# One exponential in forty by a polynomial on VectorE and GpSimd, in a four-layer attention kernel

## The chip, the cores and the metric

The kernel runs on one core of a Trainium2 chip. A core has a matrix engine (PE, TensorE), a vector engine (DVE, VectorE), an activation engine (ACT, ScalarE), a general engine (POOL, GpSimd) and a queue that issues transfers (SP). Each works through its own list of instructions in order and waits for the others by semaphores. The metric is device time in microseconds (us), the median of several runs.

## What is computed

The input `x` is 2048 tokens by 1024 features in bf16. Four layers follow one another, each with a layer norm and a residual add: A, B, A, B, with the same weights for both A and for both B.

```
x = x + A(layernorm(x));  x = x + B(layernorm(x));  x = x + A(layernorm(x));  x = x + B(layernorm(x))

A: q, k, v = split(x @ wqkv)                       # 32 heads of 32
   phi(t) = [softmax(t @ w_phi), softmax(-(t @ w_phi))]
   o = phi(q) (phi(k)^T v) / (phi(q) sum(phi(k)) + 1e-6);   return o @ wo
B: scores = q k^T / sqrt(32)                       # 32 heads, 2048 x 2048 each
   p = softmax(scores);   return (p v) @ wo
```

Layer B is full attention: per layer 32 x 2048 x 2048 exponentials. The kernel does not subtract a row's maximum; it sums `exp(scores)` by a product with ones, in the same matmuls that sum `exp(scores) v`, and divides at the end.

## The kernel before

All order is written by a planner in the program itself. Every instruction, or small group of them, is an `op` with an engine, an assumed duration, dependencies, buffers and a priority (a number; a smaller one goes first). `Sched.run` (line 143) plays these out: whenever an engine is free, it takes the ready op of smallest priority whose buffers can be had. The order that results is then emitted, and on the chip each engine follows it whatever the true durations are. Buffers come from one arena in SBUF, with a limit on how many of each class may live (`QUOTA`, line 245), and from the eight banks of PSUM.

**The two A layers** are done per chunk of 512 tokens: keys and their state (`a_keys`, line 569), then queries (`a_queries`, 708), the output product with the residual add (`a_out`, 783; the add is line 792) and the layer norm for B (`layernorm`, 441). The layer norm squares the chunk on ScalarE (line 454), lets PE average `x` and its squares by a product with a matrix of 1/1024 (line 397), and normalizes on VectorE (lines 487 and 491). For three chunks of the second A layer this is done beside the first attention, with squares on VectorE (`alone`).

**Attention** (`attention`, line 908) is a run of 2048 units for each B layer. A unit is one matmul of scores (line 937): 128 keys by 512 queries of one head, over 32 rows of PE, one bank of PSUM. Units go in 32 turns (`turns`, line 1029): turn = a chunk of 512 queries `qc` and a group of four heads `g`; in it `pp` (2), `d` (8 blocks of keys) and `j` (4) give 64 units. Three units at a time fill half of the six score banks; one ScalarE instruction takes the exponential of all three (line 943) into a buffer of class `E`, of which five may live. PE then multiplies each by `v` and by ones (line 972) and accumulates over the 16 blocks of keys in bank 6. Bank 6 is single: when a `pp` is done, VectorE copies it out (line 986) before the next may begin. At the end of a turn two transfers swap halves, and VectorE takes reciprocals (line 1016) and multiplies (line 1020).

Bank 7 (`FIL`) is the eighth bank. Through it go, beside attention, the projections that later turns need (keys, queries, values: `b_k`, `b_q`, `q_away`, `b_v`; VectorE empties the bank, lines 816, 824, 840), the output products (`b_o`, `b_last`) and, in the first attention, three chunks of the next A layer's keys. Where PE has been busy less than 75% of the last 3.4 us of the plan, the planner puts in a padding matmul to bank 7 (line 1177), if bank 7 is free and no projection uses it.

GpSimd makes two memsets (line 662) and 64 small casts (line 607), none of them in the second attention.

The factor 1/sqrt(32) is applied where VectorE copies `q` out of PSUM (lines 824 and 840).

Of the kernel before, what the change touches and what calls it, by code (L numbers as in the profile page):

```python
# [12 lines left out]
BF16 = mybir.dt.bfloat16  # L13
F32 = mybir.dt.float32

EPS_LN = 1e-5
# [16 lines left out]
class Op:  # L33
    __slots__ = ("eng", "dur", "lat", "fn", "bufs", "prio", "mode", "ndep", "out", "t", "start", "seq")

    def __init__(self, eng, dur, lat, fn, bufs, prio, mode, seq):
        self.eng, self.dur, self.lat, self.fn, self.bufs = eng, dur, lat, fn, bufs
        self.prio, self.mode, self.seq = prio, mode, seq
        self.ndep, self.out, self.t, self.start = 0, [], 0.0, None

# [5 lines left out]
class Sched:  # L46
    def __init__(self, sbuf_bytes, quota):
        self.ops = []
        self.quota = quota
        self.live = {}  # L50
        self.free = [(0, sbuf_bytes)]
        self.bank_used = [False] * 8
        self.peak = 0
        self.total = sbuf_bytes
        self.queue = {}
        self.idle = None

# [85 lines left out]
    def run(self):  # L143
# [17 lines left out]
        front = 0  # L161
        recent = []
        started = {}
        for o in self.ops:
# [3 lines left out]
        while left:  # L168
            moved = False
            for e in engines:  # L170
                if busy[e] > t + 1e-9 or not ready[e]:
                    continue
                skipped = []
                pick = None
                while ready[e] and len(skipped) < 60:
                    item = heapq.heappop(ready[e])
                    if item[0] <= todo[front] + WINDOW and self._alloc(item[2].bufs):
                        pick = item[2]
                        break
                    skipped.append(item)  # L180
                for s in skipped:
                    heapq.heappush(ready[e], s)
                if pick is None and e == "PE" and self.idle is not None and self.live.get("S", 0):

                    recent = [r for r in recent if r[1] > t - SPELL]
                    worked = sum(r[1] - max(r[0], t - SPELL) for r in recent)
                    if worked < KEEP * SPELL and not self.live.get("fil", 0) and not self.bank_used[7]:
                        pick = Op("PE", MM, LAT["PE"], self.idle, (Buf("ps", 0, "idle", [(7,)]),), 0.0, "c", 0)
                        pick.bufs[0].left = 1
                        self.queue["idle"] = [list(pick.bufs), 0]  # L190
                        assert self._alloc(pick.bufs)
                        left += 1
                if pick is None:
                    continue
                if e == "PE":
                    recent.append((t, t + pick.dur))
                d = pick.dur
                if pick.mode is not None:
                    if mode[e] is not None and mode[e] != pick.mode:
                        d += SWITCH  # L200
                    mode[e] = pick.mode
                pick.start = t
                if pick.fn is not self.idle:
                    started[pick.prio] = started.get(pick.prio, 0) + 1
                while front < len(todo) - 1 and started.get(todo[front], 0):
                    started[todo[front]] -= 1
                    front += 1
                busy[e] = t + d
                order.append(pick)
                left -= 1  # L210
                moved = True
                n += 1
                heapq.heappush(events, (t + d, n, pick, True))
                n += 1
                heapq.heappush(events, (t + d + pick.lat, n, pick, False))
            if moved:
                continue
            if not events:
                stuck = [(o.prio, o.eng, [(b.cls, b.at) for b in o.bufs]) for e in engines for _, _, o in ready[e]][:8]
                raise AssertionError(f"nothing can start at {t:.1f}: {left} left, {stuck}, live {self.live}")  # L220
            t = events[0][0]
            while events and events[0][0] <= t + 1e-9:
                _, _, o, own = heapq.heappop(events)
                if not own:
                    for b in o.bufs:
                        b.left -= 1
                        if b.left == 0:
                            self._release(b)
                for x in o.out:

                    if own != (x.eng == o.eng and x.eng not in ("SP", "AQ")):
                        continue
                    x.ndep -= 1
                    if x.ndep == 0:
                        heapq.heappush(ready[x.eng], (x.prio, x.seq, x))
# [11 lines left out]
         "lnt": 6, "lnw": 2, "lnw1": 1, "eq": 8, "ns": 4, "cw": 6, "hl": 6, "oc": 2, "slab": 7, "slabk": 3, "fin": 4,  # L247
         "rs": 8, "pkf": 1, "part": 8, "w2r": 1}
SPELL = 3.4
KEEP = 0.75  # L250


# [4 lines left out]
def dve_us(n):  # L257
    return n / 960 + 0.15
# [6 lines left out]
def kernel(  # L265
# [18 lines left out]
    assert D == 1024 and S % C512 == 0  # L284
    inv_sqrt_dh = float(DH**-0.5)

# [15 lines left out]
    onesD = const.tile([P, P], BF16, tag="onesD")  # L302
    ones_bf = const.tile([P, DH], BF16, tag="ones")
    J_bf = const.tile([P, P], BF16, tag="J")
    ident = const.tile([P, P], BF16, tag="ident")
# [8 lines left out]
    nc.vector.memset(onesD[:], 1.0 / D)  # L314
    nc.vector.memset(ones_bf[:], 1.0)
    nc.vector.memset(J_bf[:], 0.0)
    nc.vector.memset(eps[:], EPS_LN)
# [122 lines left out]

    def layernorm(c, prio, banks, alone=False):

# [5 lines left out]
        parts = [deps_x(c)[2 * i:2 * i + 2] for i in range(4)]  # L448
        for h in range(2 if alone else 4):
            hs = slice(4 * h, 4 * h + 4)  # L450
            if not alone:
                hs = slice(2 * h, 2 * h + 2)
                halves.append(op(
                    "ACT", act_us(1024), lambda hs=hs: nc.scalar.activation(  # L454
                        out=xv()[:, hs, :], in_=xT[:, hs, csl(c)], func=ACT.Square),
                    parts[h], [xb], prio))
            else:
# [6 lines left out]
        if not alone:  # L464
            mb.with_ = (qb,)
        m = mmgroup(mb, mv, lambda po: onesD[:], lambda po: xT[:, po, csl(c)], (), parts, [], prio)
        q = mmgroup(qb, qv, lambda po: onesD[:], lambda po: xv()[:, po, :], [m],
                    [halves[0], None, halves[1], None] if alone else halves, [xb], prio + 0.01)
        if alone:
# [348 lines left out]
    def b_q(g, c, prio, w, banks):  # L818
# [5 lines left out]
        cp = op("DVE", dve_us(512), lambda: nc.vector.tensor_scalar(  # L824
            out=q_v()[:, 0, :], in0=pv(), scalar1=inv_sqrt_dh, scalar2=None, op0=ALU.mult), [m], [pb, q_b], prio)
        return q_b, q_v, q_swap(q_b, q_v, cp, prio)
# [6 lines left out]
    def q_away(g, c, prio, w, banks):  # L833
# [6 lines left out]
        cp = op("DVE", dve_us(512), lambda: nc.vector.tensor_scalar(  # L840
            out=a_v(), in0=pv(), scalar1=inv_sqrt_dh, scalar2=None, op0=ALU.mult), [m], [pb, a_b], prio)
        return dma(prio, lambda: nc.sync.dma_start(out=qd_v[:, c - 2, g, :], in_=a_v()), [cp], [a_b], kb=128)
# [64 lines left out]

    def attention(base, kT, vT, q_of, gate):

# [4 lines left out]
        ]  # L914
        first = {}
        ex_of, e_of = {}, {}
        n = 0
        i = 0
        while i < len(units):
# [14 lines left out]
            def sfn(grp=grp, s_v=s_v):  # L934
# [8 lines left out]
            ex = op("ACT", act_us(w * C512), lambda s_v=s_v, e_v=e_v, w=w: nc.scalar.activation(  # L943
                out=e_v()[:, 0:w * C512], in_=s_v(), func=ACT.Exp), [so], [s_b, e_b], prio - 3)
            for x, u in enumerate(grp):
# [5 lines left out]
        if True:  # L951
            for qc, g in turns:
                T = []
                end = (qc, g) == turns[-1]
                for pp in range(2):
                    a_b, a_v = ps("acc", [(6,)])
                    last = None
                    for d in range(8):
                        prio = base + 10 * pos[(qc, g)] + 5 * pp + 0.5 * d
                        for u in range(2):  # L960
# [18 lines left out]
                            if e_of[us[1]][0] is not ebs[0]:  # L979
                                ebs.append(e_of[us[1]][0])  # L980
                            last = op("PE", 0.225, fn, flat([last, ex_of[us[0]], ex_of[us[1]], v_done[kc % 4]]),
                                      [a_b, v_b, *ebs], prio - 1, mode="c")
                    if end and pp:
                        break
# [67 lines left out]
    for layer in range(2):  # L1052
# [13 lines left out]
        for c in chunks:  # L1066
            xnA[c] = layernorm(c, base + 10 * c - 9 if base + c else -16.0, ANY)
            a_keys(c, base + 10 * c, wk_s, wv_s, kv, ANY)
# [47 lines left out]
        for g in range(G):  # L1116
            pr = at + 10 * pos[(0, g)]
            w = slab("w2", pr - 11, B_w[:, :, g * P:(g + 1) * P], P) if g else wq0
            for qc in range(NC):
# [3 lines left out]
                else:  # L1123
                    away = q_away(g, qc, pr + 2 + 6 * (qc - 2), w, FIL)
                    q_of[(qc, g)] = q_back(g, qc, at + 10 * pos[(qc, g)] - 12, away)
        oTs, last_s = attention(at, kT, vT, q_of, gate)
        if last:
# [50 lines left out]
    sch.idle = idle  # L1178

    for o in sch.run():  # L1180
        o.fn()
# [30 lines left out]
```

## Time and profile before

| | us |
|---|---|
| median of 3 runs | 2554.63 |
| lowest and highest | 2552.54, 2556.16 |
| the profiled execution | 2554.77 |
| its span, first to last instruction | 2553.0 |

| stretch of the span | what | PE busy | DVE busy | ACT busy | POOL busy |
|---|---|---|---|---|---|
| 0 to 400 | first A layer | 361 | 291 | 189 | 13 |
| 400 to 1363 | first attention | 881 | 408 | 945 | 10 |
| 1363 to 1618 | rest of the second A layer | 240 | 171 | 130 | 3 |
| 1618 to 2542 | second attention | 843 | 269 | 915 | 0 |
| 2542 to 2553 | last output rows | 4 | 6 | 1 | 0 |

The mean granted clock of TensorE is 0.985 of full speed. Times are microseconds from the first instruction, and busy time is the time in which at least one instruction of that engine ran. PE's ends are modelled and padding matmuls count as busy, so its share says little; ScalarE's and VectorE's can be read as they stand. In a line of a group the columns are: line, engine, operation, output and inputs, shapes, count, then busy time and mean duration in ns, then the idle time just before these instructions and what ended it. In a timeline the columns are start, duration, engine, line, operation.

### The profile page before, as it was taken

The numbers are of one execution on the slowest core, as the hardware profiler recorded it, in microseconds if no ns is written. First come the engines' busy times: TensorE is split into PE (matmuls) and PEld (weight loads), VectorE is DVE, ScalarE is ACT, GpSimd is POOL, SyncE is SP. The second block draws the span as 40 slices with busy tenths as digits, with TensorE's granted clock in tenths as the row PEclk, the third lists the DMA queues.
The fourth block names the chain that finished last, engine by engine and source line by source line (L and its number), as shares of the span: only waits on it lengthen the run. The fifth ranks groups of instructions, "written<-read, shape, count | busy, mean of one in ns | idle before, by whom it ended". The sixth has DMA issues, their size and how long they took to land.

```text
span 2553.0 us, 60236 instructions
## 1 busy us (share of the span) xinstructions
PE 2329.9 (91%) x26714; PEld 882.9 (35%) x26780; DVE 1144.7 (45%) x1632; ACT 2181.1 (85%) x1945; POOL 25.8 (1%) x72
## 2 busy tenths in 40 slices
PE   6899999999898998899898999999998898889888
PEld 3443443333322333333333344333332233333333
DVE  5997653333322245655646766333333222212124
ACT  5325647999999999999996555799999999999998
POOL 0000000000000000000000000000000000000000
PEclk9999999999998999999999999999999899999999
DMA  9020011111121222222323001111121011001000
GB/s 215 1 75 1 5 38 46 35 35 44 40 64 38 53 53 70 75 64 69 117 71 102 1 5 38 36 45 35 37 67 30 20 33 43 20 18 33 18 20 26
DMA packets 185270, 117.21 MB, mean 46 GB/s; under 512 B 103345, under 2 KB 175025, under 8 KB 184241
## 3 DMA queue, kind: packets, MB, share of 16 engines
q1 hardware_dynamic: 183952, 111.26, 16.3%
q8 instruction: 209, 3.42, 0.6%
q10 hardware_dynamic: 1056, 2.10, 0.2%
q14 instruction: 53, 0.43, 0.1%
HBM read 62.46 MB, written 15.73 MB: 31 GB/s over the span
## 4 chain that ended last, share of the span: by engine, by line
ACT 53%; PE 26%; issue 11%; DVE 8%; SPq 1%; DMA 1%; ACTq 0%; DVEq 0%; another core or an unknown queue 0%
ACT arena L943 51%; PE psum L397 13%; PE psum L401 4%; PE psum L972 3%; PE psum L937 3%; DVE arena L593 2%; DVE arena L602 1%; PE psum L757 1%; DVE arena L491 1%; DVE arena L487 1%; ACT arena L589 1%; SPq L432 1%; DVE arena L596 1%; DVE arena L639 0%; PE psum L702 0%
## 5 line engine op out<-in xcount | busy, mean ns | idle before, releaser
L943 ACT ACTIVATE arena<-psum 128x1536 bf16<-128x1536 f32 (+1 forms) x1366 | 1844.4, 1560 | 29.1 <-PE psum L937 23.6
L972 PE MATMUL psum<-arena 128*32 128x512 bf16 x4096 | 712.7, 390 | 13.5 <-ACT arena L943 11.6
L972 PE MATMUL psum<-arena,ones_bf 128*32 128x512 bf16 x4096 | 714.1, 391 | 0.0
L937 PE MATMUL psum<-arena 32*128 32x512 bf16 x4096 | 537.8, 387 | 135.5 <-ACT arena L943 127.3
L401 PE MATMUL psum<-arena 128*32 128x512 bf16 x8256 | 582.5, 382 | 13.8 <-DVE arena L840 2.1
L397 PE MATMUL psum<-arena 128*128 128x512 bf16 x1973 | 468.6, 382 | 26.5 <-DVE arena L491 5.5
L937 PEld LDWEIGHTS <-arena 32*128 32x128 bf16 x4096 | 181.7, 91 | 643.8 <-issue 632.1
L401 PEld LDWEIGHTS <-arena 128*32 128x32 bf16 x8256 | 213.0, 96 | 222.1 <-issue 74.2
L397 PEld LDWEIGHTS <-arena 128*128 128x128 bf16 x2032 | 193.2, 98 | 268.5 <-issue 50.2
L986 DVE COPY arena<-psum 128x512 f32<-128x512 f32 x126 | 86.9, 690 | 431.3 <-PE psum L972 428.0
L972 PEld LDWEIGHTS <-arena 128*32 128x32 bf16 x4096 | 167.7, 94 | 283.0 <-issue 259.3
L1016 DVE RECIPROCAL arena<-arena 128x128 f32<-128x128 f32 x248 | 212.8, 913 | 85.7 <-DMA arena<-arena 82.8
L816 DVE CAST arena<-psum 128x512 bf16<-128x512 f32 x112 | 77.4, 691 | 283.5 <-PE psum L401 280.3
L972 PEld LDWEIGHTS <-ones_bf 128*32 128x32 bf16 x4096 | 162.1, 94 | 70.1 <-issue 58.7
L401 PE MATMUL psum<-xT,onesD 128*32 128x512 bf16 x2172 | 179.7, 382 | 0.6 <-DVE xT L876 0.3
L589 ACT ACTIVATE arena<-psum 128x512 bf16<-128x512 f32 x80 | 42.6, 603 | 110.7 <-PE psum L397 58.8
L454 ACT ACTIVATE arena<-xT 128x1024 bf16<-128x1024 bf16 x52 | 54.6, 1060 | 73.2 <-DVE xT L792 59.2
L719 ACT ACTIVATE arena<-psum 128x512 bf16<-128x512 f32 x128 | 69.8, 598 | 38.2 <-PE psum L397 32.2
L602 DVE TENSOR_TENSOR arena<-psum,arena 128x1024 bf16<-128x1024 f32 x64 | 78.3, 1224 | 43.6 <-PE psum L401 39.4
L1020 DVE TENSOR_TENSOR arena<-arena 64x512 bf16<-64x512 f32 x124 | 85.0, 686 | 10.1 <-PE psum L972 5.7
L487 DVE TENSOR_TENSOR arena<-xT,arena 128x1024 f32<-128x1024 bf16 x64 | 77.7, 1218 | 22.7 <-ACT arena L476 22.4
L593 DVE TENSOR_REDUCE arena<-arena 128x32 f32<-128x1024 bf16 x64 | 77.6, 1213 | 19.1 <-ACT arena L589 15.0
(89 smaller groups left out, 1051.8 us busy)
## 6 DMA issues: line engine op xcount, KB each, us to landing
arena<-arena SPq DMA_DIRECT2D x124, 128.0 KB, 2.3
arena<-in_A_wqkv_dram SPq DMA_DIRECT2D x10, 1024.0 KB, 5.7
arena<-in_B_wqkv_dram SPq DMA_DIRECT2D x32, 256.0 KB, 3.3
arena<-arena SPq DMA_DIRECT2D x256, 32.0 KB, 1.9
arena<-in_B_wo_dram SPq DMA_DIRECT2D x32, 256.0 KB, 3.1
arena<-wd_k SPq DMA_DIRECT2D x8, 1024.0 KB, 6.1
arena<-in_A_wo_dram SPq DMA_DIRECT2D x4, 1024.0 KB, 6.5
arena<-in_B_wqkv_dram SPq DMA_DIRECT2D x4, 1024.0 KB, 5.5
```

What stands on the lines that cost most here:

```text
L397: nc.tensor.matmul(out_, lhsT=lhsT, rhs=rhs, start=start, stop=stop, skip_group_check=True)
L401: nc.tensor.matmul(out_[ks, :], lhsT=lhsT[:, ks], rhs=rhs, start=start, stop=stop, tile_position=(0, 32 * k), skip_group_check=True)
L487: s1 = op("DVE", dve_us(1024), lambda pr=pr, w_v=w_v: nc.vector.tensor_tensor(out=w_v(), in0=xT[:, pr, csl(c)], in1=m_v().unsqueeze(1).to_ ...
L593: red = op("DVE", dve_us(1024), lambda ev=ev, sv=sv: nc.vector.reduce_sum(out=sv(), in_=ev().rearrange("p s (h d) -> p (s h) d", d=DH), ax ...
L602: ml = op("DVE", dve_us(1024), lambda vpv=vpv, wv_=wv_, sv=sv: nc.vector.tensor_tensor(out=wv_()[:, :, :, 0:DH], in0=vpv().rearrange("p (h ...
L816: return op("DVE", dve_us(512), lambda: nc.vector.tensor_copy(out=dst(), in_=src()), [dep], bufs, prio)
L937: nc.tensor.matmul(out=s_v()[:, x * C512:(x + 1) * C512], lhsT=kT[g][1]()[r, pp, d * P:(d + 1) * P], rhs=q_of[(qc, g)][1]()[r, (pp + j // ...
L943: ex = op("ACT", act_us(w * C512), lambda s_v=s_v, e_v=e_v, w=w: nc.scalar.activation(out=e_v()[:, 0:w * C512], in_=s_v(), func=ACT.Exp), ...
L972: nc.tensor.matmul(out=a_v()[col:col + 32, :], lhsT=v_v()[:, kc % 4, o:o + DH] if what == 0 else ones_bf[:], rhs=ev()[:, x * C512:(x + 1) ...
L986: cp = op("DVE", dve_us(512), lambda t_v=t_v, a_v=a_v: nc.vector.tensor_copy(out=t_v(), in_=a_v()), [last], [a_b, t_b], prio - 4)
L1016: rc = [op("DVE", 128 * 8 / 960 + 0.12, lambda b=b, d_v=d_v, r_v=r_v: nc.vector.reciprocal(out=r_v()[:, b * P:(b + 1) * P], in_=d_v()[:, b ...
L1020: s = [op("DVE", dve_us(512), lambda a=a, b=b, k=k, o_v=o_v, r_v=r_v, T=T: nc.vector.tensor_tensor(out=o_v()[a, :], in0=T[k][1]()[a, :], i ...
```

## The change

It has four parts.

**Part of the exponentials moves.** In some turns, for some pairs of blocks of keys (`d`, `d+1`), the unit with `j = 3` is taken out of the run and done by the new function `exp_dve`. `EXTRA` says which: in the first attention one pair in each of turns 10 to 19 (20 units), in the second two pairs in each of turns 11 to 29, and three in the odd ones above 16 (90 units). The scores go to bank 7. VectorE adds a constant that rounds the score to a multiple of a quarter and takes the difference (two instructions for each unit, from PSUM), and builds the power of two from the rounded part (two instructions for the pair, the second writes integers). GpSimd evaluates a monic polynomial of the difference in three steps, each an addition and a product over 128x1024 in fp32. VectorE adds the last constant and multiplies. The pair's priority is 7 below that of its use (ten are one turn), and new buffer classes limit how many are under way: `xs` 1, `xu`, `xg`, `xx` 3 each, `E1` 4. The polynomial is one of leading coefficient 1 whose result has the same scale as ScalarE's, so the instructions on ScalarE take no correcting bias.

**The scale of q.** `q` is scaled by 1/(4 sqrt(32) ln 2), so that a quarter of a score is a power of two; ScalarE's exponential gets the factor 4 ln 2 as its scale.

**Layer norm by halves.** Where ScalarE squares, it does so in two instructions of 2048 elements and not in four of 1024 (except in the second A layer's one chunk), and both, like the averaging matmuls, wait for the whole chunk. Twelve layer norms change.

**Padding while bank 7 is held.** Where PE has little to do and bank 7 is in use, the planner may now put in four matmuls that add zero to the running sum in bank 6 (`idle_acc`), as long as a sum is open there.

```diff
+         "xs": 1, "xu": 3, "xg": 3, "xx": 3, "E1": 4}
+ROUND = 1.5 * 2**21
+LEAD = 7.0
+EXTRA = (lambda i: [(i % 2, 2)] if 10 <= i < 20 else [],
+         lambda i: ([(0, 2), (0, 5), (1, 4)] if i % 2 and i > 16 else [(0, 2), (1, 2)]) if 11 <= i < 30 else [])
...
-                    if worked < KEEP * SPELL and not self.live.get("fil", 0) and not self.bank_used[7]:
+                    if worked >= KEEP * SPELL:
+                        pass
+                    elif self.bank_used[7]:
+                        if accum:
+                            pick = Op("PE", MM, LAT["PE"], self.idle_acc, (), 0.0, "c", 0)
+                            left += 1
+                    elif not self.live.get("fil", 0):
...
-    inv_sqrt_dh = float(DH**-0.5)
+    q_scale = float(DH**-0.5 / (4 * math.log(2)))
...
-    def layernorm(c, prio, banks, alone=False):
+    def layernorm(c, prio, banks, alone=False, n=2):
...
-        for h in range(2 if alone else 4):
-            hs = slice(4 * h, 4 * h + 4)
+        for h in range(n):
+            hs = slice(8 // n * h, 8 // n * h + 8 // n)
...
-                    "ACT", act_us(1024), lambda hs=hs: nc.scalar.activation(
+                    "ACT", act_us(4096 // n), lambda hs=hs: nc.scalar.activation(
                         out=xv()[:, hs, :], in_=xT[:, hs, csl(c)], func=ACT.Square),
-                    parts[h], [xb], prio))
+                    parts[h] if n == 4 else deps_x(c), [xb], prio))
...
-    def attention(base, kT, vT, q_of, gate):
+    def exp_dve(qc, g, pp, d, prio, kT, q_of):
+        u_b, u_v = sb("xu", 2, C512, dt=F32)
+        g_b, g_v = sb("xg", 2, C512, dt=F32)
+        x_b, x_v = sb("xx", 2, C512, dt=F32)
+        e_b, e_v = sb("E1", 2, C512)
+        r = slice(96, 128)
+        gs = []
+        for k in range(2):
+            s_b, s_v = ps("xs", FIL)
...
+            uo = op("DVE", dve_us(512), lambda k=k, s_v=s_v: nc.vector.tensor_scalar(
+                out=u_v()[:, k, :], in0=s_v(), scalar1=POW2_D, scalar2=ROUND, op0=ALU.add, op1=ALU.add),
+                [so], [s_b, u_b], prio + 0.01)
+            gs.append(op("DVE", dve_us(512), lambda k=k, s_v=s_v: nc.vector.scalar_tensor_tensor(
+                out=g_v()[:, k, :], in0=u_v()[:, k, :], scalar=ROUND, in1=s_v(), op0=ALU.subtract, op1=ALU.subtract),
+                [uo], [s_b, u_b, g_b], prio + 0.01))
+        wo = op("DVE", 1024 / 1920 + 0.15, lambda: nc.vector.tensor_scalar(
+            out=u_v(), in0=u_v(), scalar1=ROUND - 31.5, scalar2=ROUND + 32.0, op0=ALU.max, op1=ALU.min),
+            gs, [u_b], prio + 0.02)
+        wo = op("DVE", 1024 / 1920 + 0.15, lambda: nc.vector.tensor_scalar(
+            out=u_v().bitcast(I32), in0=u_v(), scalar1=ROUND - 31.75, scalar2=float(2**25),
+            op0=ALU.subtract, op1=ALU.mult), [wo], [u_b], prio + 0.02)
+        last = gs
+        for i, c in enumerate(POW2_C):
+            last = [op("POOL", 1.1, lambda i=i, c=c: nc.gpsimd.tensor_scalar(
+                out=x_v(), in0=(x_v() if i else g_v()), scalar1=c, scalar2=None, op0=ALU.add),
+                last, [g_b, x_b], prio + 0.02)]
+            last = [op("POOL", 2.25, lambda: nc.gpsimd.tensor_tensor(
+                out=x_v(), in0=x_v(), in1=g_v(), op=ALU.mult), last, [g_b, x_b], prio + 0.02)]
+        eo = op("DVE", dve_us(1024), lambda: nc.vector.scalar_tensor_tensor(
+            out=e_v(), in0=x_v(), scalar=POW2_0, in1=u_v(), op0=ALU.add, op1=ALU.mult),
+            [wo, *last], [x_b, u_b, e_b], prio + 0.02)
+        return eo, (e_b, lambda: e_v().rearrange("p a b -> p (a b)"))
+
+    def attention(base, kT, vT, q_of, gate, extra):
...
+        for qc, g in turns:
+            for pp, d in extra(pos[(qc, g)]):
+                eo, (e_b, e_v) = exp_dve(qc, g, pp, d, base + 10 * pos[(qc, g)] + 5 * pp + 0.5 * d - LEAD, kT, q_of)
+                for k in range(2):
+                    ex_of[(qc, g, pp, d + k, 3)] = eo
+                    e_of[(qc, g, pp, d + k, 3)] = (e_b, e_v, k)
+        units = [u for u in units if u not in ex_of]
...
-                out=e_v()[:, 0:w * C512], in_=s_v(), func=ACT.Exp), [so], [s_b, e_b], prio - 3)
+                out=e_v()[:, 0:w * C512], in_=s_v(), func=ACT.Exp, scale=4 * math.log(2)),
+                [so], [s_b, e_b], prio - 3)
...
-            xnA[c] = layernorm(c, base + 10 * c - 9 if base + c else -16.0, ANY)
+            xnA[c] = layernorm(c, base + 10 * c - 9 if base + c else -16.0, ANY, n=4 if layer else 2)
...
+    def idle_acc():
+        for k in range(4):
+            nc.tensor.matmul(psum[32 * k:32 * k + 32, 6 * C512:7 * C512], lhsT=zero[:], rhs=xT[:, 0, 0:C512],
+                             start=False, stop=False, tile_position=(0, 32 * k), skip_group_check=True)
+    sch.idle_acc = idle_acc
```

## The prediction, made before the kernel was run

> **What bounds the kernel now.** I read the page's busy shares first, then its chain, then the groups, then the engines by stage.
>
> ```profile
> PE 2329.9 (91%) x26714; PEld 882.9 (35%) x26780; DVE 1144.7 (45%) x1632; ACT 2181.1 (85%) x1945; POOL 25.8 (1%) x72
> ...
> ACT 53%; PE 26%; issue 11%; DVE 8%; SPq 1%; DMA 1%; ACTq 0%; DVEq 0%; another core or an unknown queue 0%
> ...
> L943 ACT ACTIVATE arena<-psum 128x1536 bf16<-128x1536 f32 (+1 forms) x1366 | 1844.4, 1560 | 29.1 <-PE psum L937 23.6
> ...
> L937 PE MATMUL psum<-arena 32*128 32x512 bf16 x4096 | 537.8, 387 | 135.5 <-ACT arena L943 127.3
> ```
>
> The reader should see that the 1366 exponentials of L943 fill 1844 us with only 29 us of idle time in front, and that the score matmuls (L937) wait for them, not they for the matmuls. By stage:
>
> ```profile
> core 0: us, PE busy (x) PEld busy (x) DVE busy (x) ACT busy (x) POOL busy (x), PEclk, DMA share, GB/s
> 1934.00:2106.00 172.00, 152.37 (x2022) 52.53 (x2018) 48.52 (x65) 170.00 (x127) 0.00 (x0) 0.96 0.10 28
> 2106.00:2479.00 373.00, 331.80 (x4454) 117.88 (x4450) 90.19 (x119) 373.00 (x279) 0.00 (x0) 1.00 0.10 26
> 689.00:978.00 289.00, 258.31 (x3251) 85.00 (x3243) 97.41 (x125) 282.86 (x211) 0.00 (x0) 0.95 0.19 48
> ```
>
> From 2106 to 2479 us ScalarE is never idle: 279 exponentials in 373 us, 1.337 us each, 0.446 us per unit, 28.5 us per turn of 64 units. VectorE works 90 of 373 us (6.9 per turn), GpSimd not at all. These three stretches are the ones that the new units lie in: turns 11 to 16 and 17 to 29 of the second attention, turns 10 to 19 of the first (attention begins at 400 and 1618 us).
>
> Two engines the change brings together already meet in this trace (timeline, VectorE and GpSimd):
>
> ```profile
> 1.24 1.80 POOL L662 MEMSET arena<- 128x2048 bf16 x1
> 1.68 1.40 DVE L322 COPY rep<-J_bf 128x32 bf16<-128x32 bf16 x1
> ...
> 1130.96 1.40 DVE L1020 TENSOR_TENSOR arena<-arena 64x512 bf16<-64x512 f32 x2
> ...
> 1130.99 0.84 POOL L607 CAST arena<-arena 128x32 bf16<-128x32 f32 x1 [6.07 <-DVE arena L596]
> ...
> 1294.09 1.23 DVE L602 TENSOR_TENSOR arena<-psum,arena 128x1024 bf16<-128x1024 f32 x1
> ...
> 1294.12 0.32 POOL L607 CAST arena<-arena 128x32 bf16<-128x32 f32 x1 [13.60 <-PE psum L937]
> ```
>
> A copy of 32 elements took 1.40 us and ended 0.04 us after GpSimd's memset. A GpSimd cast that takes 0.32 us took 0.84 beside a VectorE instruction with two SBUF inputs, and 0.32 beside one that reads PSUM and SBUF. So some VectorE instructions and GpSimd's shut each other out.
>
> **The change part by part.** The profiled execution took 2554.77 us (span 2553.0), 0.14 above the median of the three runs; I sum against it.
>
> *ScalarE.* In the first attention 10 pairs leave (20 units), in the second 12 turns x 2 + 7 x 3 = 45 pairs (90 units). Groups of three: 683 become 676, and 683 become 653. 37 x 1.337 = -49.5 us, all on the path, since the idle time there is near zero. The factor in the exponential's scale argument costs nothing: scale is already an operand of L589, whose 128x512 takes 603 ns against 598 for L719.
>
> *VectorE.* Per pair: two instructions PSUM to SBUF, 0.69 each (L824's row: 691 ns); two of SBUF and PSUM, 0.69 to 0.75 (L477 686, L687 751); two scalar instructions 128x1024 SBUF to SBUF in fp32, 0.69 if two elements go per cycle as in L686 (512 in 425 ns), 1.22 if one (L487); I take 0.69, the like kind; the last with two SBUF inputs, 1.22 to 1.28, I take 1.25. Sum 5.45 us, 300 us in all. In turns 17 to 29 that is 33 x 5.45 = 180 us beside 90, in some 341 us: hidden by VectorE's idle time while its waits stay under 70 us. What stands behind such a wait in VectorE's queue is the copy of the accumulator (L986): bank 6 is single, PE's next accumulation waits for it, and the next scores stand behind that in PE's queue. ScalarE has one set of scores ready, so a PE wait over some 1.3 us reaches it.
>
> *GpSimd.* Three adds and three products of 128x1024 fp32. No row has them. Memsets of 128 and 2048 elements took 204 and 1843 ns, 0.854 ns per element plus 0.09, so one pass over 1024 takes 0.97 us; a product that moves two inputs and an output one after another would take three passes, 2.72. The add: 0.97 to 1.8. The program books 1.1 and 2.25, inside these bounds; its entries for rows that exist are near (cast 0.3 against 0.338, memset 2.0 against 1.843, 1536 exponentials 1.344 against 1.337), so I take them: 10.05 us per pair, 0 on the path if GpSimd keeps up. The Trainium skill (GPSIMD Engine Reference, 3.1 Elementwise — side-by-side cycle accounting) gives 4497 ns for such an instruction over 2048 elements; half of it, an estimate, is 2.25 and gives the sum below; no run here shows it.
>
> *The meeting of the two.* By the rows above, the two fp32 scalar instructions, the last instruction and L1020 (0.69, twice a turn) exclude GpSimd's: a pair then needs 10.05 + 2 x 0.69 + 1.25 = 12.7 us of whatever they share. Turns 17 to 29 need 33 pairs and 13 x 1.4 us of L1020, 437 us. ScalarE's time for them is 7 x 58 + 6 x 60 units, 341 us, 335 to the last use. The buffers allow four finished pairs ahead (E1) and three in work; turns 11 to 16 ask for two pairs in 26.7 us (25.4 + 1.4), so the lead can form before; I count 5.5 pairs, 70 us. Late by 437 - 70 - 335 = +32 us. PE waits for the exponentials in its fixed order, and the scores behind them wait too. Bounds: 0 (at 11.5 us per pair, a product of 1.87, the lead covers all) to +102 (no lead). The first attention asks for one pair in 27.6 us: 0.
> The Trainium skill (SBUF — State Buffer, Who interferes with whom) says that the pair of ports is an exclusive lock for the whole instruction, taken by VectorE in its two-port modes and, against reads, with two SBUF inputs. Read so, the sum is the one below; without it, 27.5 x 10.05 = 276 us fit into 335 and the time would be 2506. The rows bear it out.
>
> *Bank 7 and PE.* Two scores per pair, 0.39 each, and bank 7 held twice for some 2 us: 45 pairs x 4 = 180 us of some 500, beside projections that are few there (L816's cast came 6 times from 2200 to 2480). Cover: the bank's idle time; without it some fillers move. 0.
>
> *Padding matmuls while bank 7 is held.* In the first attention's stretch ScalarE is short by 6 us (282.86 of 289) with the clock at 0.95; in the second's by 2. Between 0 and -8; I take -3, since part of these gaps will have another cause.
>
> *Layer norm.* Twelve of the thirteen on ScalarE go from four squares to two, all after the last residual add. The first attention's last norm, in the timeline:
>
> ```profile
> 379.58 0.69 DVE L792 TENSOR_TENSOR xT<-xT,psum 128x512 bf16<-128x512 bf16 x1 [1.04 <-PE psum L397]
> 380.31 1.06 ACT L454 ACTIVATE arena<-xT 128x1024 bf16<-128x1024 bf16 x1 [2.40 <-DVE xT L792]
> ...
> 383.56 0.68 DVE L477 TENSOR_TENSOR arena<-psum,arena 128x512 f32<-128x512 f32 x1
> ```
>
> Its last add ends at 380.3; now one square of 1.06 follows, then two of 1.06 + 0.87 = 1.93, the second half of whose matmuls follows: +1.6 to +2.8 us, and this norm is on the path, twice: +4. The other six of the stages are covered by the next chunk's queries (without this +2 each), the first four by the weights' folding (0 to +3). ScalarE saves 12 x 0.38 = 4.6, off the path. Bounds -4 to +15. The zero tile and the q factor: 0.
>
> Sum: 2554.8 - 49.5 + 32 - 3 + 4 = 2538.
>
> **The rivals.**
> (1) *GpSimd keeps up*: products under 1.87 us, or the exclusion touches only part of an instruction. For it: GpSimd is idle all through attention, VectorE three quarters. Against it: the 1.40 us copy. Time 2554.8 - 49.5 + 1 = 2506.
> (2) *Slower: the shared port becomes the bound.* Mechanism: as above, with a lead of two pairs only, because the fixed order starts a pair 0.7 turns ahead of its use and a q tile must be there. Then 31 x 12.7 + 18 - 335 = +77 and the time is 2583; it decides where the lead is under 4.1 pairs, or at my lead where a pair costs over 13.4 us. For it: two turns of five pairs ask 66 us of the port, against 52.6 of ScalarE now and 57 before. Against it: the quotas allow the lead, and part of an instruction's fixed time need not hold the port.
> (3) *It comes out even*: late VectorE copies hold bank 6, 38 times at about 1.2 us, on top of what is counted: +45 - 30; about 2553.
>
> **How the numbers follow.** Forecast (2520 to 2549) 0.40; rival 1 (2500 to 2520) 0.24; rival 2 (2560 to 2600) 0.25; rival 3 0.11. About 0.2% (5 us) is what a measurement of this kernel can tell from no change. Faster: 0.40 + 0.24 = 0.64; within 0.2% 0.09; slower, with the rest of rival 3, 0.27. The range leaves out rival 1's fastest end and the slowest part of rival 2: 2503 to 2583; the forecast's own is 2520 to 2549.
>
> **What would show it.** Right: 1329 exponentials of L943's kind; GpSimd products near 2.25 us, longer beside VectorE's two-input instruction; VectorE's fp32 scalar instructions well over 0.69 in the mean; PE's accumulations waiting for VectorE's last instruction, and idle ScalarE, in turns 17 to 29 and not in the first attention. Wrong: ScalarE still fully busy there (rival 1), or idle from turn 11 on (rival 2); a first attention that is not about 9 us shorter would make the ScalarE term wrong.

## The result and the profile after

The changed kernel takes 2829.99 us in the median of 4 runs (2826.82 to 2831.36), against 2555.39 for the kernel before on the same chips. The ratio is 1.1075, with a 95% interval from 1.1055 to 1.1094: 275 us slower, where 17 us faster was forecast. The profiled execution took 2826.82 us, its span 2825.0.

From the page of the changed kernel, the busy shares and the groups that answer to those of before, and GpSimd's two new ones:

```profile
PE 2455.0 (87%) x27576; PEld 886.7 (31%) x27576; DVE 1534.0 (54%) x2018; ACT 2149.2 (76%) x1884; POOL 901.7 (32%) x402
...
L1014 ACT ACTIVATE arena<-psum 128x1536 bf16<-128x1536 f32 x1329 | 1815.5, 1515 | 362.1 <-PE psum L1008 158.1
L963 POOL TENSOR_SCALAR arena<-arena 128x1024 f32<-128x1024 f32 x165 | 481.9, 2920 | 1224.1 <-ACT arena L1014 614.0
...
L966 POOL TENSOR_TENSOR arena<-arena 128x1024 f32<-128x1024 f32 x165 | 395.3, 2396 | 13.8
```

The 37 exponentials are gone from ScalarE (1329 are left), but it now idles 362 us in front of them, not 29. GpSimd's additions (L963) take 2.92 us each, the products (L966) 2.40. By stage (same columns as before the change: length, then busy us of PE, weight loads, VectorE, ScalarE, GpSimd, then the granted clock):

```profile
640.00:990.00 350.00, 299.39 (x3870) 96.63 (x3866) 157.43 (x196) 301.62 (x224) 149.94 (x57) 0.93 0.17 43
...
2110.00:2480.00 370.00, 263.30 (x3039) 77.58 (x3039) 218.79 (x239) 245.42 (x177) 333.64 (x126) 0.81 0.07 19
```

In the second attention GpSimd is busy 334 of 370 us and ScalarE 245: the bound has moved to GpSimd. In the first attention, with one pair per turn, GpSimd is busy less than half of the time, and ScalarE still loses 48 of 350 us. I count an attention from its seventh exponential, with which the steady run has begun in every version. So counted, the first attention goes from 392 to 1397 us (405 to 1363 before), the second from 1654 to 2813 (1623 to 2541 before).

The chain between 2300 and 2340 us is GpSimd's own queue and almost nothing else (start, duration, what):

```profile
by line: POOL arena L963 54.7%; POOL arena L966 48.1%; issue 2.6%
...
2311.18 2.36 POOL arena L966
2313.54 0.08 issue
2313.62 3.10 POOL arena L963
```

How that reaches ScalarE is in the list of waits (who waited for whom, us, times, longest):

```profile
DVE arena L968 <- POOL arena L966: 271.8, 55, 8.9
...
PE psum L1044 <- DVE arena L1059: 69.7, 21, 7.2
...
PE psum L1044 <- DVE arena L968: 51.6, 13, 7.1
...
ACT arena L1014 <- PE psum L1008: 158.1, 112, 9.4
...
ACT arena L1014 <- DVE arena L968: 72.8, 25, 6.5
...
ACT arena L1014 <- POOL arena L966: 52.5, 16, 6.1
...
ACT arena L1014 <- PE psum L1044: 51.4, 42, 5.9
```

VectorE's last instruction of a pair (L968) stands at its planned place in VectorE's queue and waits there 4.9 us for GpSimd, 55 times. Behind it stands the copy that frees bank 6 (L1059, L986 before the change); PE's accumulations (L1044) wait for both, and the next scores stand behind them. The trace bears the order out: in 62 of the 69.7 us that PE waits for a copy, an L968 that had itself waited is among the four VectorE instructions in front of that copy.

The last four lines are ScalarE's own waits. 158 us of them end when scores arrive (L1008), which is the path just named. Another 125 us end with L968 or with a GpSimd product (L966) directly, although an exponential needs neither result. What it shares with them is the arena: in the plan its output buffer may be given a place that a moved pair has released, and then a late pair holds up the exponential itself. This second path is inferred from the program and these waits; no run takes it away by itself.

### The profile page after: what moved, and what is told of

Same layout as the page of the kernel before. It is cut to its first block, busy times and chain, and to the rows that moved or that the text cites. A ratio compares the mean times of both kernels' runs of the same rounds, so it can differ in the third digit from the quotient of the medians.

```text
span 2825.0 us, 62729 instructions
## 1 busy us (share of the span) xinstructions
PE 2455.0 (87%) x27576; PEld 886.7 (31%) x27576; DVE 1534.0 (54%) x2018; ACT 2149.2 (76%) x1884; POOL 901.7 (32%) x402
## 5 line engine op out<-in xcount | busy, mean ns | idle before, releaser
L1014 ACT ACTIVATE arena<-psum 128x1536 bf16<-128x1536 f32 x1329 | 1815.5, 1515 | 362.1 <-PE psum L1008 158.1
L963 POOL TENSOR_SCALAR arena<-arena 128x1024 f32<-128x1024 f32 x165 | 481.9, 2920 | 1224.1 <-ACT arena L1014 614.0
L1044 PE MATMUL psum<-arena 128*32 128x512 bf16 x4096 | 744.9, 409 | 140.9 <-DVE arena L1059 69.7
L1044 PE MATMUL psum<-arena,ones_bf 128*32 128x512 bf16 x4096 | 746.4, 410 | 0.0
L425 PE MATMUL psum<-arena 128*32 128x512 bf16 x8256 | 588.2, 387 | 44.6 <-DVE arena L847 10.7
L1008 PE MATMUL psum<-arena 32*128 32x512 bf16 x3986 | 544.3, 402 | 81.0 <-ACT arena L1014 76.8
L966 POOL TENSOR_TENSOR arena<-arena 128x1024 f32<-128x1024 f32 x165 | 395.3, 2396 | 13.8
L1008 PEld LDWEIGHTS <-arena 32*128 32x128 bf16 x3986 | 150.8, 91 | 628.9 <-issue 618.3
L1044 PEld LDWEIGHTS <-arena 128*32 128x32 bf16 x4096 | 168.5, 96 | 322.8 <-issue 299.1
L968 DVE SCALAR_TENSOR_TENSOR arena<-arena 128x1024 bf16<-128x1024 f32 x55 | 90.5, 1645 | 271.8 <-POOL arena L966 271.8
L1255 PE MATMUL psum<-xT,zero 128*32 128x512 bf16 x2608 | 236.4, 427 | 0.0
L1044 PEld LDWEIGHTS <-ones_bf 128*32 128x32 bf16 x4096 | 162.3, 96 | 191.4 <-issue 181.0
L1059 DVE COPY arena<-psum 128x512 f32<-128x512 f32 x126 | 86.5, 687 | 102.2 <-PE psum L1044 98.8
L949 DVE TENSOR_SCALAR arena<-psum 128x512 f32<-128x512 f32 x110 | 75.7, 689 | 88.5 <-PE psum L944 76.1
L612 ACT ACTIVATE arena<-psum 128x512 bf16<-128x512 f32 x80 | 42.7, 601 | 85.5 <-PE psum L421 57.2
```

Source lines behind the costliest of these rows:

```text
L425: nc.tensor.matmul(out_[ks, :], lhsT=lhsT[:, ks], rhs=rhs, start=start, stop=stop, tile_position=(0, 32 * k), skip_group_check=True)
L963: last = [op("POOL", 1.1, lambda i=i, c=c: nc.gpsimd.tensor_scalar(out=x_v(), in0=(x_v() if i else g_v()), scalar1=c, scalar2=None, op0=AL ...
L966: last = [op("POOL", 2.25, lambda: nc.gpsimd.tensor_tensor(out=x_v(), in0=x_v(), in1=g_v(), op=ALU.mult), last, [g_b, x_b], prio + 0.02)]
L968: eo = op("DVE", dve_us(1024), lambda: nc.vector.scalar_tensor_tensor(out=e_v(), in0=x_v(), scalar=POW2_0, in1=u_v(), op0=ALU.add, op1=ALU ...
L1008: nc.tensor.matmul(out=s_v()[:, x * C512:(x + 1) * C512], lhsT=kT[g][1]()[r, pp, d * P:(d + 1) * P], rhs=q_of[(qc, g)][1]()[r, (pp + j // ...
L1044: nc.tensor.matmul(out=a_v()[col:col + 32, :], lhsT=v_v()[:, kc % 4, o:o + DH] if what == 0 else ones_bf[:], rhs=ev()[:, x * C512:(x + 1) ...
```

## The experiments

My theory after the result was that GpSimd's additions are the cause: 2.77 us each where nothing disturbs them, in an order laid for 1.1. Rival A was the exclusion, that is, that VectorE and GpSimd shut each other out; rival B was the two parts that move no unit (the norm and the padding). Each ratio is to runs of the kernel before on the same chip (2554.3 to 2555.4 in the median).

| kernel | us | ratio to before, 95% |
|---|---|---|
| the changed kernel | 2829.99 | 1.1055 to 1.1094 |
| true_prices | 2716.12 | 1.0616 to 1.0645 |
| add_forms | 2683.98, one run | |
| norm_only | 2550.13 | 0.9975 to 0.9992 |
| no_adds | 2548.60 | 0.9967 to 0.9989 |
| pad_only | 2545.75 | 0.9955 to 0.9980 |
| rest_only | 2539.78 | 0.9926 to 0.9951 |
| fewer_pairs | 2526.08 | 0.9876 to 0.9903 |
| vector_only | 2504.94 | 0.9793 to 0.9820 |
| no_scalar | 2502.51 | 0.9771 to 0.9803 |
| vector_more | 2500.61 | 0.9772 to 0.9799 |
| no_gpsimd | 2490.77 | 0.9736 to 0.9765 |

### rest_only: everything but the moved units

```diff
-EXTRA = (lambda i: [(i % 2, 2)] if 10 <= i < 20 else [],
-         lambda i: ([(0, 2), (0, 5), (1, 4)] if i % 2 and i > 16 else [(0, 2), (1, 2)]) if 11 <= i < 30 else [])
+EXTRA = (lambda i: [], lambda i: [])
```

> The changed kernel with no unit moved: layer norm by halves, the scale of q and the padding in bank 6 stay. Theory (the loss is GpSimd's add of 2.77 us where the order was laid for 1.1): 2545 to 2562, about as the kernel before. Rival A (VectorE and GpSimd shut each other out at the SBUF port): the same. Rival B (the padding or the norm delays PE): most of the 275 us stays, over 2650.

2539.8 us: rival B falls, and more: these parts gain 15 us, below the range that I gave. All that the moved units do is to be counted from 2540.

### no_adds: the same order without GpSimd's additions

```diff
-            last = [op("POOL", 1.1, lambda i=i, c=c: nc.gpsimd.tensor_scalar(
-                out=x_v(), in0=(x_v() if i else g_v()), scalar1=c, scalar2=None, op0=ALU.add),
-                last, [g_b, x_b], prio + 0.02)]
+            last = [op("POOL", 1.1, lambda: None, last, [g_b, x_b], prio + 0.02)]
...
-                out=x_v(), in0=x_v(), in1=g_v(), op=ALU.mult), last, [g_b, x_b], prio + 0.02)]
+                out=x_v(), in0=g_v(), in1=g_v(), op=ALU.mult), last, [g_b, x_b], prio + 0.02)]
```

> The changed kernel in the same order of instructions, but GpSimd's three additions are left out (its three products, still of two SBUF inputs, stay, so the polynomial is not computed). Theory: a pair takes GpSimd 3 x 2.4 = 7.3 us, less than the 10.05 that the order was laid for, so VectorE's last instruction waits little and ScalarE's saving shows: 2505 to 2530. Rival A: VectorE's instructions still meet products nearly as often, so a good part of the loss stays: 2600 to 2700. Rival B: over 2650.

2548.6 us. The order is untouched, and with the additions 281 us are gone, of the 290 that the changed kernel lies above rest_only: the theory holds for the bulk. But 2549 lies between the two expectations: ScalarE's saving still did not show, although GpSimd was busy only 207 of 380 us from 2100 on. In these groups of no_adds (line, engine, operation, shapes, count, busy us, mean ns of one) VectorE's instructions have grown:

```profile
L958 DVE TENSOR_SCALAR arena<-arena 128x1024 int32<-128x1024 f32 x55 | 108.9, 1979 | 1.7
L1091 DVE TENSOR_TENSOR arena<-arena 64x512 bf16<-64x512 f32 x124 | 96.7, 779 | 7.0 <-PE psum L1042 2.8
L966 DVE SCALAR_TENSOR_TENSOR arena<-arena 128x1024 bf16<-128x1024 f32 x55 | 96.1, 1748 | 3.6 <-PE psum L1042 2.8
...
L955 DVE TENSOR_SCALAR arena<-arena 128x1024 f32<-128x1024 f32 x55 | 50.4, 915 | 1.6
```

### no_gpsimd and no_scalar: the exclusion

As in no_adds, the moved exponentials are not computed; the kernels ask only what the instructions cost. no_gpsimd leaves the products out as well, no_scalar leaves the products and leaves out VectorE's two scalar instructions; both keep the order.

```diff
 no_gpsimd
...
+            last = [op("POOL", 1.1, lambda: None, last, [g_b, x_b], prio + 0.02)]
+            last = [op("POOL", 2.25, lambda: None, last, [g_b, x_b], prio + 0.02)]
...
-            out=e_v(), in0=x_v(), scalar=POW2_0, in1=u_v(), op0=ALU.add, op1=ALU.mult),
+            out=e_v(), in0=u_v(), scalar=POW2_0, in1=u_v(), op0=ALU.add, op1=ALU.mult),
 no_scalar (on top of no_adds)
...
+        wo = op("DVE", 1024 / 1920 + 0.15, lambda: None, gs, [u_b], prio + 0.02)
+        wo = op("DVE", 1024 / 1920 + 0.15, lambda: None, [wo], [u_b], prio + 0.02)
```

> The changed kernel in the same order, but all six GpSimd instructions of a pair are left out (the polynomial is not computed; VectorE's last instruction, still with two SBUF inputs, reads the power of two twice). It asks why no_adds came to 2549 although GpSimd had time to spare. Theory (exclusion at the SBUF port: in no_adds VectorE's second fp32 scalar instruction took 2.27 us in the median against 0.69): without GpSimd it is 0.69 again and the time falls to 2490 to 2510, that is 2540 less 110 x 0.446. Rival (VectorE's own added work or the order of the plan holds ScalarE back): 2530 to 2550.

> no_adds (GpSimd's additions left out) with VectorE's two fp32 scalar instructions of each pair left out too, in the same order; GpSimd's products and VectorE's last instruction with two SBUF inputs stay (the power of two is not built). no_adds was 2549, no_gpsimd 2491. If these two scalar instructions are what the products shut out (they were 84 us longer in no_adds than their shortest): 2491 to 2510. If it is the last instruction and L1020's kind with two SBUF inputs: 2525 to 2549.

no_gpsimd: 2490.8 us, which is rest_only less 49.0. ScalarE's saving is whole, and VectorE's added work by itself costs nothing. The same groups in no_gpsimd:

```profile
L965 DVE SCALAR_TENSOR_TENSOR arena<-arena 128x1024 bf16<-128x1024 f32 x55 | 66.8, 1215 | 5.6 <-PE psum L1041 2.5 <-issue 1.6 <-PE psum L425 0.8
...
L958 DVE TENSOR_SCALAR arena<-arena 128x1024 int32<-128x1024 f32 x55 | 38.1, 693 | 1.7
L955 DVE TENSOR_SCALAR arena<-arena 128x1024 f32<-128x1024 f32 x55 | 38.1, 692 | 1.6
```

The second scalar instruction is 0.69 us here and 1.98 in no_adds, where GpSimd runs nothing but products. So the products alone cost 58 us (2549 - 2491). They do so by lengthening VectorE's instructions and not by late results: in no_adds VectorE idles only 3.6 us in front of the last instruction of a pair (L966). no_scalar: 2502.5, so 46 of the 58 go with the two scalar instructions. The other 12 are left, and there the two kinds with two SBUF inputs are still 0.29 and 0.14 us longer than in no_gpsimd; no run takes these apart from other causes.

### true_prices and fewer_pairs: the order and GpSimd's rate

```diff
-            last = [op("POOL", 1.1, lambda i=i, c=c: nc.gpsimd.tensor_scalar(
+            last = [op("POOL", 2.95, lambda i=i, c=c: nc.gpsimd.tensor_scalar(
...
-            last = [op("POOL", 2.25, lambda: nc.gpsimd.tensor_tensor(
+            last = [op("POOL", 2.5, lambda: nc.gpsimd.tensor_tensor(
 fewer_pairs, besides:
-         lambda i: ([(0, 2), (0, 5), (1, 4)] if i % 2 and i > 16 else [(0, 2), (1, 2)]) if 11 <= i < 30 else [])
+         lambda i: ([(0, 2), (1, 2)] if i % 2 else [(0, 4)]) if 11 <= i < 30 else [])
```

> The changed kernel with the planner's entries for GpSimd set to 2.95 and 2.5 us, near what the changed kernel's trace has; the same pairs, so the order is laid anew. Theory: GpSimd still has 45 pairs x 16.4 = 740 us to do where ScalarE needs some 500, so it stays slower, but what the wrong order cost comes back: 2690 to 2740. If the order costs nothing, 2830 stays. Rival A: the exclusion is no part of the entries, so little changes: over 2800.

> As true_prices, but in the second attention's turns 11 to 29 two pairs in odd turns and one in even (29 pairs, not 45). Theory: GpSimd needs 1.5 x 16.4 = 25 us per turn, below ScalarE's 27; 39 pairs in all, 78 units x 0.446 = 35 us saved less some 5: 2520 to 2540, faster than before. Rival A: the port's exclusion still delays VectorE's copies: 2560 to 2620.

true_prices: 2716.1 us. The same work in an order laid for nearly its true durations takes 114 us less. Nearly all of the first attention's loss is in this: it lasts 955 us there, 1005 in the changed kernel and 946 in no_gpsimd. The second lasts 1096, 1159 and 879; what true_prices keeps there over no_gpsimd, 217 us, goes with GpSimd's rate. Its stage from 2106 to 2479 us:

```profile
2106.00:2479.00 373.00, 326.98 (x4676) 121.87 (x4668) 231.82 (x246) 242.99 (x179) 363.31 (x137) 0.97 0.07 20
```

The same stage of vector_only (below), where GpSimd does nothing:

```profile
2106.00:2479.00 373.00, 348.30 (x4926) 123.55 (x4926) 245.77 (x301) 372.92 (x278) 0.00 (x0) 1.00 0.10 26
```

In true_prices GpSimd is busy 363 of 373 us. The granted clock is 0.97 with PE busy 327 of 373 us, where the changed kernel had 0.81 with PE busy 263 of 370. The low clock is not what held ScalarE: with the better clock it is no busier (0.65 of the time against 0.66). That the clock fell because PE waited is likely, but no run tests it. fewer_pairs: 2526.1, as expected: a rate that GpSimd can hold makes the moved units gain 13.7 us over rest_only, of the 34.8 that 78 units are worth (78 x 0.446).

### add_forms: what an addition costs

```diff
+                if i == 0:
+                    nc.gpsimd.tensor_scalar(out=x_v()[:, 0, :], in0=g_v()[:, 0, :], scalar1=c, scalar2=None, op0=ALU.add)
+                elif i == 1:
+                    nc.gpsimd.tensor_tensor(out=x_v(), in0=x_v(), in1=g_v(), op=ALU.add)
+                else:
+                    nc.gpsimd.tensor_scalar(out=x_v(), in0=x_v(), scalar1=c, scalar2=None, op0=ALU.mult)
```

> The changed kernel with GpSimd's three additions replaced, to price their forms: an addition of a constant over 512 elements, an addition of two tensors over 1024, a product with a constant over 1024 (the polynomial is not computed). If an instruction with a constant costs a fixed sum: the one over 512 takes over 2 us. If it costs by the element: about 1.4 us. If the constant is what costs, the addition of two tensors takes 2.35 us like the product. The time: 2700 to 2790, since a pair still needs 13.6 us of GpSimd where the order was laid for 10.05.

Durations in ns, least, median and greatest, of the three forms in this order, and of the products:

```profile
L965 POOL TENSOR_SCALAR arena<-arena x55: 1485/1495/2655, 652.3 to 2592.0; 128x512 f32<-128x512 f32 x55
...
L967 POOL TENSOR_TENSOR arena<-arena x55: 2347/2677/2817, 657.5 to 2595.6; 128x1024 f32<-128x1024 f32 x55
...
L969 POOL TENSOR_SCALAR arena<-arena x55: 2774/3093/3634, 662.7 to 2601.2; 128x1024 f32<-128x1024 f32 x55
...
L971 POOL TENSOR_TENSOR arena<-arena x165: 1892/2357/2877, 655.1 to 2604.1; 128x1024 f32<-128x1024 f32 x165
```

By the least durations (1.485 and 2.774 us) the price goes by the element: 512 more cost 1.29 us, 2.5 ns each. That leaves some 0.2 us as the fixed part, an estimate from two sizes. Whether the constant is added or multiplied does not matter (2.77 at least); a second tensor in its place is cheaper, 2.35 at least. The time, 2684 in a single run, is a little under the range that I gave.

### norm_only and pad_only: the 15 us

```diff
 norm_only (on top of rest_only)
-                        if accum:
+                        if False:
 pad_only (on top of rest_only)
-    def layernorm(c, prio, banks, alone=False, n=2):
+    def layernorm(c, prio, banks, alone=False, n=4):
...
```

> No unit moved and no padding in bank 6; layer norm by halves and the scale of q stay. rest_only was 15 us faster than before. If the norm does it (attention begins 23 and 28 us earlier there): 2538 to 2546. If the padding does: 2550 to 2560, as my price of +4 for the norm would have it.

> No unit moved and layer norm as before; the padding in bank 6 and the scale of q stay. If the norm made the 15 us: 2550 to 2556 (my price for the padding was -3, bounds 0 and -8). If the padding did: 2538 to 2546.

Neither makes the 15 us alone: norm_only is 4.1 us faster than before, pad_only 8.5. They add to 12.6; the 2 us that are missing lie within the intervals of the three runs. With the padding alone the first attention lasts 953 us and the second 916, against 958 and 919 before, and ScalarE's idle time in front of its exponentials falls from 29 to 20 us. That agrees with the 8 us that ScalarE was short of in the two stretches of the prediction.

In rest_only the last residual add of the first query stage ends at 369.4 us, not at 380.3, and in norm_only it ends at 369.5: with the norm changed the planner puts the stage in another order. The steady run of exponentials begins 12 us earlier in rest_only (393.3 against 404.9, the seventh exponential), and the first attention ends 15 us earlier (1348.2 against 1363.0). The 23 and 28 us of the expectation are counted from the fifth exponential; in rest_only that one runs ahead of a gap of 13 us, in the kernel before it comes behind the gap, so those figures are no head start.

### vector_only and vector_more: the steps on VectorE

```diff
+                last = [op("DVE", dve_us(1024), lambda i=i, c=c: nc.vector.scalar_tensor_tensor(
+                    out=x_v(), in0=(x_v() if i else g_v()), scalar=c, in1=g_v(), op0=ALU.add, op1=ALU.mult),
+                    last, [g_b, x_b], prio + 0.02)]
 vector_only: the pairs of fewer_pairs; vector_more:
+         lambda i: ([(0, 2), (1, 2)] if i >= 17 else [(0, 4)]) if 9 <= i < 31 else [])
```

> The moved units without GpSimd: VectorE does each of the three steps in one instruction (add and multiply, two SBUF inputs, about 1.22 us), with the pairs of fewer_pairs (39). Theory: VectorE has 9.1 us per pair and, without the exclusion, no waits; rest_only's 2540 less most of 78 x 0.446 = 35: 2505 to 2520, faster than fewer_pairs (2526). Rival: what a pair costs beside ScalarE is not the exclusion but VectorE's load in front of the bank 6 copies: 2526 to 2545.

> vector_only with 46 pairs and not 39: in the second attention one pair in each of turns 9 to 16 and two in each of 17 to 30. Seven pairs more are 14 x 0.446 = 6 us less if VectorE keeps up (two pairs ask 25 of 26.7 us in a turn): 2498 to 2503. If VectorE is the bound by then: 2505 to 2520.

vector_only: 2504.9 us, all of the 34.8 that 78 units are worth below rest_only's 2539.8, and 21 below fewer_pairs, which moves the same units. So even at a rate that GpSimd can hold its part costs 21 us; the runs do not divide them between the exclusion and waits for late results. One VectorE instruction of 1.22 us does a step that took GpSimd 5.1. vector_more: 2500.6, the fastest version found that computes the whole, 2.1% below the kernel before (ratio 0.9785, 0.9772 to 0.9799). Its last seven pairs gain 4.3 of 6.2 us.

## Why the prediction was wrong

**What bounds the kernel, and the ScalarE term (-49.5): right.** no_gpsimd, with 110 units moved and nothing late, is 49.0 us below rest_only. The prediction wanted a first attention about 9 us shorter as the sign: 946 us against rest_only's 955.

**GpSimd: the step that failed.** "The add: 0.97 to 1.8. The program books 1.1 and 2.25, inside these bounds; its entries for rows that exist are near ... so I take them". The product was right (2.34 where nothing disturbs it). The addition takes 2.77, above the upper bound. The lower bound came from memsets, which read nothing; and entries that fit casts, memsets and exponentials say nothing of an instruction that had not run in this kernel. By no_adds the additions cost 281 us in this order. The Trainium skill (GPSIMD Engine Reference, 4.1 Engine selection) says that one-input work is roughly line-rate on GpSimd; the trace does not agree: with one input it took 2.5 ns per element here, more than with two.

**The meeting of the two (+32): GpSimd does fall behind, but by far more, for the same price.** A pair needs about 16.4 us (3 x 2.92 + 3 x 2.40 + six gaps of 0.08), not 12.7. Two pairs then ask 33 us of turns that last 26.7, so "the lead can form before" fails too. For the 45 pairs: 45 x 16.4 + 19 x 1.4 = 765 us, where ScalarE's time for turns 11 to 29 is 502 (1126 units). An estimate by the same sum, with the 15 us of rest_only, is 2554.8 - 49.5 - 15 + 263 = 2753, and some 27 less if the pairs start a turn ahead. true_prices measured 2716. The other 114 us up to 2830 are the order's.

**The order was missing from the sum.** The prediction gave the first attention 0, as 12.7 us fit into 27.6, and expected no idle ScalarE there. With 16.4 they still fit, and yet it became 59 us longer than in no_gpsimd. What is late there is each pair against its place in a fixed order: VectorE waits at L968 with the copies for bank 6 behind it. true_prices takes 50 of these 59 back without moving a unit less. The prediction named this queue and let VectorE's waits pass "while its waits stay under 70 us"; at L968 alone they were 144 us in turns 17 to 29, the stretch that it meant, and 272 in all.

**The exclusion: borne out, dearer for VectorE than for GpSimd.** The Trainium skill (SBUF — State Buffer, Who interferes with whom) has an exclusive lock for the whole instruction; the trace agrees: L958 took 2.75 us beside a product that began 0.5 us before it. The prediction counted the time that GpSimd loses. In the changed kernel that is small (the mean addition is 0.15 us over its undisturbed 2.77), while VectorE's four kinds of instructions grew by 107 us in all over their shortest. The prediction expected the scalar instructions "well over 0.69", but gave their growth no price, as hidden by VectorE's idle time. That is a second step that failed: in no_adds, with no addition at all and GpSimd busy only 207 of 380 us, this growth costs 58 us. Even with additions at no cost the kernel takes 2549 us, the upper end of the forecast's own range, so the sum was short by more than the one price.

**The norm (+4) and the padding (-3):** -4.1 and -8.5. For the norm, the work after the last add did grow (12.6 us to the last normalizing instruction before, 17.1 in rest_only); what I left out is that the planner lays the whole stage anew, and that the last add then comes 11 us earlier. The padding came out at the end of its bounds.

**The rivals.** Rival 2 comes nearest: the bound moved to GpSimd's side, at 2830 and not 2583. The test that it named, late from turn 11 on, is met: ScalarE was busy 62 of 80 us from 1930 on. But its mechanism, a shared port and a short lead, was not needed: 45 pairs at the undisturbed durations, 15.8 us each, ask 711 us of GpSimd alone, and ScalarE's time is 502. Rival 2 too used 12.7 us per pair, so its price and the range's upper end shared the error of the forecast. Rival 1 asked for products under 1.87 us or a weaker exclusion, and neither is the case. Rival 3's late copies of bank 6 are there too (PE waited 69.7 us for them, 21 times).

## What to carry to other kernels

Where a plan fixes the order of an instruction that no trace has shown, its price deserves one measurement before any sum: here an addition of 2.77 us, booked at 1.1, brought in 281 us of cost, where the moved units were worth 49. Compare the engine that gets the work with what it can hold per turn, and read its queue as well as its load, because a late result in a fixed order stops whatever stands behind it, even where the engine is half idle. Here GpSimd cost VectorE time wherever VectorE ran fp32 scalar instructions or read two SBUF inputs; the same steps on VectorE, which had time to spare, were four times as fast and gave the whole of what the moved units are worth (39 pairs in vector_only).

## What was not expected of the hardware

GpSimd's instruction with a constant operand is slower than with a second tensor: 2.77 us against 2.34 for 128x1024 in fp32 (and 1.49 for 128x512). An fp32 scalar instruction of VectorE, 0.69 us alone, took 2.27 in the median in no_adds. The timeline there shows one such meeting, VectorE first and then GpSimd:

```profile
2302.27 0.69 DVE L955 TENSOR_SCALAR arena<-arena 128x1024 f32<-128x1024 f32 x1
2302.99 2.27 DVE L958 TENSOR_SCALAR arena<-arena 128x1024 int32<-128x1024 f32 x1
2305.18 2.91 DVE L966 SCALAR_TENSOR_TENSOR arena<-arena 128x1024 bf16<-128x1024 f32 x1
...
2302.36 7.48 POOL L964 TENSOR_TENSOR arena<-arena 128x1024 f32<-128x1024 f32 x3 [5.37 <-ACT arena L1012]
```

The first scalar instruction and GpSimd's first product wait for the same result of VectorE, so they start together, the second scalar instruction waits out the product, and the instruction behind it waits out the next one. The exclusion is no matter of chance there: the dependencies bring the two engines together, and in 45 of the 55 pairs the second scalar instruction took over 1.5 us.
